# Routed experts behind a thresholded attention: rows stored unnormalized with their factors, low parts moved to GpSimd, a search with fewer steps per level, and a later turning of rows

## The chip, the cores and the metric

One Trainium2 chip, one of its cores. The metric is the device time of one execution in microseconds (us). Engines are named as the profile names them: PE is TensorE (PEld its weight loads), DVE is VectorE, ACT is ScalarE, POOL is GpSimd, SP is SyncE, which here only issues DMAs. Each engine runs its own instruction stream in order.

## The reference

```python
scores = scale * q @ k.T                                  # 8 batches, 8 heads, 576 rows, head size 64
scores = where(scores >= max(scores) - tau, scores, -1e9)
attn   = softmax(scores);  x = (attn @ v) as rows         # 4608 rows of 512
logits = x @ w_gate                                       # 8 experts
for idx in argsort(-logits.flatten()):                    # greedy, each expert takes at most 576 rows
    if row not assigned and expert not full: assign
out[mask_e] = relu(x[mask_e] @ w1[e]) @ w2[e]             # w1[e]: 512x1024, w2[e]: 1024x512
```

With 4608 rows and eight experts of 576 every expert ends full. The kernel finds, round by round, the expert that fills at the highest threshold, its 576 rows, and closes it.

## The kernel before

**Attention** (L23 to L328) goes through 32 pairs of heads of a batch: scores, maximum, exponential, mask with row sums, transposes, product with v. The result of a batch stays as XT (features by rows), not yet divided by the row sums; `rd_calc` and `rd_unit` form the reciprocals (RD). `xt_unit` (L202) turns one tile of 128 rows (64 for c=4) with four transposes on PE into a PSUM bank of `bank_v` (two banks), and `ev` (L209) multiplies each row's eight heads by their reciprocals and stores the tile in `xrows` in DRAM by SP. For batches 0 and 1 DVE multiplies from PSUM (L213). For the other six the ACT copies and POOL multiplies (L219), or, for the tile c=4, ACT does eight small scalings (L217). These 30 units run after the attention (L323 to L327): a loop that keeps a clock of its own puts one unit every XTY=1.05 into the streams, and between them the steps of the first expert's search.

**Router** (L370 to L576). A search level compares the best logit of each row with 32 (or 16) levels (`step_cmp`, L415; DVE), counts per expert on PE (`step_cnt`), flags the levels at which some expert is full (`step_flag`), and sums the flags on PE into the next lower bound (`step_n`, L437). There are seven levels, lv from -1 to 5. From lv 1 on a level adds a multiple of a step to the bound: tile E2, made by DVE from `st`, the bound and the sum in PSUM, is compared in the next level. `pick` and `pick2` find the expert: the one-hot matrix is masked, summed on DVE, summed over partitions on PE, and the first expert with a count of CAP or more is taken. `rank1`, `rank2`, `pack` give the list of rows (`idx`); `close` takes the expert and its rows out of the logits.

**Experts** (`moe`, L582). `run` holds jobs (generators) with due times; an expert's matmuls (`ffn`, L661) advance its clock, and whatever falls due is written into the streams between two matmuls. All numbers are split into a high part (fp32r) and the low rest, and three products are summed. Jobs of expert r are `w1_load` (L593: load, high part on ACT, low part w1l on DVE), `w2_load` (L617), `rows` (L634: gather of five tiles by POOL's indirect DMA after `idx`, then per tile four transposes on PE, high part xh on ACT, low part xl on DVE) and the search of the next expert (`place`, L704), which starts for r>2 once the second layer of expert r-3 is done. In `ffn` the first layer makes eight blocks of 128 features (PSUM, relu into `hf` on ACT, high part into H on ACT, low part in `low`, L678); the low part is on POOL for experts in LOWP=(0,1), else on DVE, and always on DVE for the last block. The second layer (L684) makes five row tiles, which POOL scatters to the output. For expert 0, `ffn` begins when half of the rows are turned ("half"), and its first block is made in two halves.

Constants of the schedule: GA (wait between gather and turning), RW (wait after each turned tile), LATS (allowance for a DVE result in a search step), each by expert.

Of the kernel before, what the change touches and what calls it, by code (L numbers as in the profile page):

```python
# [19 lines left out]
PPB=8; LTB=1; VTB=5; HOLD=1; CAPV=3.3; RATE=(2.4,2.4); NBO=2; XAC=(4,); NDEF=4; XTB=4; XTY=1.05; XT0=2.0; XRB=2  # L20


def attention(ctx, tc, qk, vl, tau, wgd, xrows, xts, Lg, nb_batches, ident, swap, R, after_first):  # L23
# [134 lines left out]
    RD={}  # L158
# [43 lines left out]
    def xt_unit(b,c):  # L202
        ps=bank_v([128,4,128])
        n=128 if c<4 else 64
        for j in range(4):
            T.transpose(ps[:n,j],XT[b][:,j,c*128:c*128+n],ident)
        if b<nb_batches-NDEF-NBO: xr=wk.tile([128,512],F32,name="xr",bufs=XRB)
        else: xr=wk.tile([128,2,S],F32,name="pp",bufs=PPB)[:,0,:512]
        def ev():  # L209
            src=RD[b][:,:,2*c:2*c+2] if c<4 else RD["m",b][0:64]  # L210
            src=src.unsqueeze(3).to_broadcast([n,4,2,64])
            xv=xr[:n].rearrange("p (j h d) -> p j h d",j=4,h=2); pv=ps[:n].rearrange("p j (h d) -> p j h d",h=2)
            if b<nb_batches-NDEF-NBO: V.tensor_tensor(xv,pv,src,op=ALU.mult)  # L213
            elif c in XAC:
                for j in range(4):
                    for h in range(2):
                        A.activation(xv[:,j,h],pv[:,j,h],AF.Copy,scale=RD[b][:n,j,2*c+h:2*c+h+1] if c<4 else RD["m",b][0:64,j,h:h+1])  # L217
            else:
                A.activation(xv,pv,AF.Copy); G.tensor_tensor(xv,xv,src,op=ALU.mult)  # L219
            nc.sync.dma_start(xrows[b*S+c*128:b*S+c*128+n,:],xr[:n])  # L220
        return ev
# [111 lines left out]
def const_arrays():  # L333
# [10 lines left out]
    put("lev",2.0**(1-5.0*np.arange(1,6)))  # L344
    put("io",np.arange(J+2)); put("io4",np.arange(J+2)/16)
# [24 lines left out]
class Router:  # L370
# [8 lines left out]
    def consts(s):  # L379
# [14 lines left out]
        s.cmp=t("cmp",[128,NC_*J],BF16); s.fl=t("fla",[128,1],BF16); V.memset(s.fl,0.0)  # L394
# [35 lines left out]
    def step_flag(s,lv):  # L430
# [4 lines left out]
        jk=s.wk.tile([32,8],F32,name="jka")  # L435
        V.tensor_scalar(jk,ps[0:32,0:8],CAP-0.5,None,op0=ALU.is_ge,op1=ALU.max,accum_out=s.fl[0:32])
    def step_n(s,B):  # L437
# [3 lines left out]
        E2=s.wk.tile([128,J+2],F32,name="E",bufs=3)  # L441
        ps=s.ps()
        if lv>0:
            s.T.matmul(ps[:,0:1],s.hb[:,lv-1:lv].to_broadcast([128,128]),s.fl,start=True,stop=True)
            if lv<5: V.scalar_tensor_tensor(E2,s.st[:,lv-1],B["lo"],ps[:,0:1].to_broadcast([128,J+2]),op0=ALU.add,op1=ALU.add)
            else: V.tensor_tensor(E2[:,:1],B["lo"],ps[:,0:1],op=ALU.add)
            return {"E":E2,"lo":E2[:,0:1],"lv":lv+1}
        n=ps[:,0:1]
        s.T.matmul(n,s.ones,s.fl,start=True,stop=True)
# [12 lines left out]
    def pick(s,E):  # L462

        V=s.V; wk=s.wk; lo=E["lo"]
        ge=wk.tile([128,NC_],BF16,name="ge"); s.ge=ge; V.tensor_scalar(ge,s.b,lo,None,op0=ALU.is_ge)
        V.tensor_tensor(s.oh,s.oh,ge.unsqueeze(2).to_broadcast([128,NC_,8]),op=ALU.mult)
        c8=wk.tile([128,8],BF16,name="c8"); s.c8=c8
        with s.nc.allow_low_precision(reason="counts up to 36 are exact"): V.tensor_reduce(c8,s.oh.rearrange("p c e -> p e c"),axis=AX.X,op=ALU.add)
    def pick2(s):
        V=s.V; wk=s.wk; ps=s.ps()  # L470
        s.T.matmul(ps[:,0:8],s.ones,s.c8,start=True,stop=True)
        f=wk.tile([128,8],F32,name="f8"); s.m=wk.tile([128,1],F32,name="m8")
        V.scalar_tensor_tensor(f,ps[:,0:8],CAP-0.5,s.w8,op0=ALU.is_ge,op1=ALU.mult)
# [63 lines left out]
    def phase(s,last=False):  # L537
# [21 lines left out]
        yield V.wait()  # L559
        held(0.13); s.pick2(); s.stage="pick"; s.rank1(E)  # L560
        yield V.wait()
        held(0.2); s.rank2()
    def pack(s,first):
# [4 lines left out]
        if first: s.warm(WARM[0])  # L568
        yield V.wait()
        held(0.7); s.compact(cps,poh,R)  # L570
        if first: s.warm(WARM[1])
        yield V.wait()
        held(0.5); s.gather4(cps)
        if first: s.warm(WARM[2])
        yield V.wait() if first else 0.35
        s.idx=s.compact2(cps)  # L576

LATS=[0.15,0.05,0.4]+[0.6]*5; FIX=(0.125,0.2)
GA=[7.0,5.5,7.5,9.0]; HALF=1; WARM=[20,4,50]
W1Y=5.0; L2O=(0,4,1,2,3); L2Z=1; HFB=3; RW=[0.2,0.6,1.0,2.0]; LOWP=(0,1); LPF=7; LOWT=1.4; PREPW=1; WLY=(1.0,1.0)  # L580

def moe(ctx,tc,R,start,xrows,w1,w2,out,ident):  # L582
# [10 lines left out]
    def w1_load(r,s):  # L593
        while r>0 and ("w1",r-1) not in done: yield 0.5
# [7 lines left out]
        s["w1h"]=w1p.tile([128,4,F],F32R,name="w1h"); s["w1l"]=w1p.tile([128,4,F],F32R,name="w1l")  # L602
        for k in range(4):
            t=s["w1s",k]
            if r==0:
                A.activation(s["w1h"][:,k],t,AF.Copy)
                while "idx" not in s: yield 0.25
                V.tensor_tensor(s["w1l"][:,k],t,s["w1h"][:,k].bitcast(F32),op=ALU.subtract)
                yield 1.1; continue
# [6 lines left out]
        done.add(("w1",r))  # L616
# [17 lines left out]
    def rows(r,s):  # L634
# [11 lines left out]
        for t in order:  # L646
# [10 lines left out]
            if t==1: done.add(("half",r))  # L657
# [165 lines left out]
```

## Time and profile before

| what | value |
| --- | --- |
| device time, three runs | 1034.92, 1032.56, 1034.87 us (median 1034.87) |
| the profiled execution | 1034.18 us, of it span 1032.4 us |
| busy PE / DVE / ACT / POOL | 980.9 / 776.4 / 640.7 / 323.7 us |
| mean granted PE clock | 0.976 |
| first matmuls of experts 0, 1, 2, 3 | 545.95, 618.10, 679.93, 739.28 us |
| last matmul | 1022.68 us |
| data moved by DMA | 113.03 MB, mean 109 GB/s |

The page gives busy time per engine and cuts the span into 40 slices. A window row says, for a stretch from a to b: its length, busy time of each engine with the number of instructions, the granted clock of PE, the share of the DMA engines and GB/s. A timeline row says: start, duration, engine, line, operation, written tile, read tiles, shapes, number of instructions merged; in brackets the idle time before it and what ended it. A group row says: line, engine, operation, tiles, shapes, count | busy time, mean duration in ns | idle time before them. Operations of DVE in the router and the experts all carry L366, the line of the helper that records them; they are told apart by their tiles.

### The profile page before, as it was taken

Reading aid. Unit: us, or ns where it says so; the run is one execution under the profiler, and the core shown is the slowest. Engines: PE = TensorE matmul, PEld = TensorE weight load, DVE = VectorE, ACT = ScalarE, POOL = GpSimd, SP = SyncE. Lnnn points to the kernel's source line nnn. Section 1 sums busy time; section 2 is a strip of 40 time slices with the busy share of each in tenths; the row PEclk is TensorE's granted clock in tenths of the full one; section 3 lists DMA queues with packets and bytes.
Section 4 is the critical chain, followed back from the end, with each engine's and each line's share of the span. In section 5 each row is a group of like instructions: output and inputs, shape, how many; then the busy total and the mean of one; then the engine's idle time right before and its main releaser. Section 6 shows DMA issues by size and latency. Waiting matters only on the chain. (4 is left out here: it accounts for less than half of the span.)

```text
span 1032.4 us, 24067 instructions
## 1 busy us (share of the span) xinstructions
PE 980.9 (95%) x9122; PEld 716.1 (69%) x9122; DVE 776.4 (75%) x2086; ACT 640.7 (62%) x1221; POOL 323.7 (31%) x485
## 2 busy tenths in 40 slices
PE   7999999999999999999768899999999999999996
PEld 4555555555555555555557779798897978889895
DVE  7999999999999999997677677767585676844230
ACT  6889888888888888886544235444352534445340
POOL 3333433333333333332653445312204021232201
PEclk9999999999999999999588999999999999999998
DMA  6321134232433222302563251504325051364101
GB/s 224 108 90 72 65 138 149 85 136 103 153 107 107 108 80 81 108 2 93 181 204 102 89 162 52 191 30 134 127 82 169 16 196 62 125 219 137 41 11 41
DMA packets 36003, 113.03 MB, mean 109 GB/s; under 512 B 4400, under 2 KB 5296, under 8 KB 35376
## 3 DMA queue, kind: packets, MB, share of 16 engines
q1 hardware_dynamic: 28496, 89.03, 24.3%
q0 software_dynamic: 5888, 18.88, 5.9%
q10 hardware_dynamic: 1504, 3.59, 1.1%
q8 instruction: 72, 1.18, 0.5%
q14 instruction: 43, 0.35, 0.1%
HBM read 89.19 MB, written 21.23 MB: 107 GB/s over the span
## 5 line engine op out<-in xcount | busy, mean ns | idle before, releaser
L76 POOL TENSOR_SCALAR nb<-nb,taub 128x1 f32<-128x1 f32 x288 | 147.4, 512 | 294.5 <-DVE z L75 223.4
L75 DVE TENSOR_SCALAR_CACHE_REDUCE z<-sc 128x576 f32<-128x576 f32 x288 | 205.9, 751 | 32.4 <-PE sc L70 31.0
L86 ACT ACTIVATE pp<-z,nb 128x576 f32<-128x576 f32 x256 | 187.3, 773 | 31.7 <-DVE z L75 30.3
L90 DVE SCALAR_TENSOR_TENSOR pp<-z,nb,pp 128x576 f32<-128x576 f32 x256 | 199.9, 813 | 0.3
L690 PE MATMUL pf<-w2h,H 128*128 128x512 f32 x576 | 196.1, 402 | 1.1 <-DVE H L366 1.1
L70 PE MATMUL sc<-qk 64*128 64x288 f32 (+1 forms) x1280 | 179.9, 426 | 2.1 <-DMA qk<-qk_dram 1.7
L145 PE MATMUL xo<-pt,vt 128*64 128x288 f32 x1024 | 151.9, 418 | 0.7 <-ACT xt L152 0.7
L114 ACT ACTIVATE pt<-tb 128x512 f32<-128x512 f32 x256 | 140.1, 594 | 13.9 <-PE tb L99 11.4
L99 PEld LDWEIGHTS tb<-ident,pp 64*128 64x128 f32 x2304 | 86.0, 139 | 71.6 <-ACT pt L114 16.7
L690 PE MATMUL pf<-w2l,H 128*128 128x512 f32 x320 | 128.2, 401 | 0.0
L697 POOL DMA_INDIRECT out_dram<-y,idx x40 | 41.9, 1048 | 265.9 <-ACT y L693 161.4
L690 PEld LDWEIGHTS pf<-w2h,H 128*128 128x128 f32 x576 | 106.3, 188 | 20.0 <-DVE H L366 1.5
L99 PE MATMUL tb<-ident,pp 64*128 64x64 f32 x2304 | 109.0, 230 | 10.1 <-ACT pt L114 6.0
L70 PEld LDWEIGHTS sc<-qk 64*128 64x128 f32 (+1 forms) x1280 | 94.4, 179 | 30.6 <-DVE pp L90 9.2
L670 PE MATMUL pf<-xh,w1h 128*128 128x288 f32 x512 | 113.5, 300 | 1.2 <-ACT xh L653 1.2
L670 PE MATMUL pf<-xh,w1l 128*128 128x288 f32 x512 | 113.9, 301 | 0.0
L670 PE MATMUL pf<-xl,w1h 128*128 128x288 f32 x512 | 113.3, 300 | 0.0
L676 ACT ACTIVATE hf<-pf 128x576 f32<-128x576 f32 x64 | 41.8, 652 | 105.7 <-PE pf L670 94.7
L145 PEld LDWEIGHTS xo<-pt,vt 128*64 128x64 f32 x1024 | 62.5, 136 | 63.5 <-issue 26.2
L693 ACT ACTIVATE y<-pf 128x512 f32<-128x512 f32 x40 | 23.9, 598 | 115.9 <-PE pf L690 99.3
L670 PEld LDWEIGHTS pf<-xh,w1h 128*128 128x128 f32 x512 | 83.1, 190 | 3.7 <-ACT xh L653 1.7
L670 PEld LDWEIGHTS pf<-xl,w1h 128*128 128x128 f32 x512 | 82.8, 189 | 0.2 <-DVE xl L366 0.2
(185 smaller groups left out, 1366.8 us busy)
## 6 DMA issues: line engine op xcount, KB each, us to landing
qk<-qk_dram SPq DMA_DIRECT2D x31, 1008.0 KB, 4.8
w2s<-w_dram SPq DMA_DIRECT2D x32, 512.0 KB, 5.6
w1s<-w_dram SPq DMA_DIRECT2D x28, 512.0 KB, 5.6
vt<-vl_dram SPq DMA_DIRECT2D x32, 320.0 KB, 5.5
xrows<-pp SPq DMA_DIRECT2D x24, 256.0 KB, 2.0
xts<-xt SPq DMA_DIRECT2D x2, 1152.0 KB, 5.2
pt<-xts SPq DMA_DIRECT2D x2, 1152.0 KB
xrows<-xr SPq DMA_DIRECT2D x8, 256.0 KB, 2.1
```

What stands on the lines that cost most here:

```text
L70: T.matmul(sc[o,f,:HS], kd["q",h][r,c], kd[k,h][r,:],start=True,stop=True)
L75: V.tensor_scalar(z,SC.pop(t)[:,:,:HS],-0.125,None,op0=ALU.mult,op1=ALU.min,accum_out=nb[:,0:1])
L76: G.tensor_scalar(nb[:,1:2],nb[:,0:1],taub[:,0:1],None,op0=ALU.add)
L86: A.activation(pview(t),ZB[t].rearrange("p a b -> p (a b)"),AF.Exp,bias=NBI[t][:,0:1],scale=-1.0)
L90: V.scalar_tensor_tensor(pv,ZB.pop(t).rearrange("p a b -> p (a b)"),NBI[t][:,1:2],pv,op0=ALU.is_le,op1=ALU.mult,accum_out=den_of(p)[:,p%4, ...
L99: g=slice(64*r,64*r+64); T.transpose(o[:,r],x[g],ident[g,g])
L114: A.activation(PT[p][:,i%2,:,(i//2)*128:(i//2+1)*128].rearrange("p k (r q) -> p r k q",r=2),tb,AF.Copy)
L145: T.matmul(xo[64*h:64*h+64,:HS],v[:,u,64*h:64*h+64],PT[p][:,h,u,q],start=(u==0),stop=False,skip_group_check=True)
L670: T.matmul(ps[:,h,:HS],s[w][:,k,f*128:(f+1)*128],s[x][:,k,h*HS:(h+1)*HS], start=(k==0 and j==0),stop=(k==3 and j==2))
L676: A.activation(hf,ps[:,:,:HS],AF.Relu)
L690: T.matmul(ps[:,0,:],H[:,f,c:c+128],s[w][:,f],start=(f==0 and j==0),stop=e)
L697: G.indirect_dma_start(out=out,out_offset=IOA(ap=s["idx"][:n,t:t+1],axis=0),in_=y[:n],in_offset=None)
```

## The change

- `xt_unit`: rows are stored as they are, 520 columns wide: 512 values and the row's eight reciprocals. Early batches: DVE copies from PSUM, POOL copies the factors. Others: two copies on ACT. POOL's multiplies and the small scalings are gone.
- `rows`: a gathered tile is multiplied by its factors, on DVE in place (for expert 0's tile of 64 rows by eight scalings on ACT), before it is turned. The scaling of tile i+1 is issued right after the turning of tile i.
- Search: from lv 2 on one `scalar_tensor_tensor` compares `st` plus the sum in PSUM with the logits, so E2 isn't formed; in its place the sum in PSUM is made of the flags of all levels so far (1 to 5 small matmuls). The bound is added to `st` once. After lv 5 the counts come with the flags, so that `pick` needs neither the masked one-hot matrix nor its sums (except for the last expert).
- Expert 0 and 1: expert 1's search starts while expert 0's rows are gathered and goes through two levels between the turnings; `close` is cut in two and stands within `pack` for experts 0 and 1; w1l of expert 0 is made after its rows, in four column pieces; the order of expert 0's products is by kind (w1h·xh, w1h·xl, w1l·xh).
- Constants: LOWP is (0,1,2,3,4,5); GA, RW and LATS as below.

```diff
+        early=b<nb_batches-NDEF-NBO
+        if early: xr=wk.tile([128,XW],F32,name="xr",bufs=XRB)
...
             src=RD[b][:,:,2*c:2*c+2] if c<4 else RD["m",b][0:64]
...
-            if b<nb_batches-NDEF-NBO: V.tensor_tensor(xv,pv,src,op=ALU.mult)
-            elif c in XAC:
...
+            if early:
+                V.tensor_copy(xv,ps[:n]); G.tensor_scalar(fv,src,1.0,0.0,op0=ALU.mult,op1=ALU.add)
             else:
-                A.activation(xv,pv,AF.Copy); G.tensor_tensor(xv,xv,src,op=ALU.mult)
+                A.activation(xv,ps[:n],AF.Copy); A.activation(fv,src,AF.Copy)
...
     def step_cmp(s,E):
+        if lv>1:
+            o=1 if lv<5 else 0
+            V.scalar_tensor_tensor(s.cmp...,s.st[:,lv-2,o:o+J]...,E["add"],s.b...,op0=ALU.add,op1=ALU.is_le)
+            return
...
     def step_flag(s,lv):
+        if lv==1: V.tensor_scalar(s.st,s.st,s.lo,None,op0=ALU.add)
...
     def step_n(s,B):
-            s.T.matmul(ps[:,0:1],s.hb[:,lv-1:lv].to_broadcast([128,128]),s.fl,start=True,stop=True)
-            if lv<5: V.scalar_tensor_tensor(E2,s.st[:,lv-1],B["lo"],ps[:,0:1].to_broadcast([128,J+2]),...)
+            for l in range(lv,0,-1):
+                k=32 if l==5 else 128
+                s.T.matmul(d,s.hb[0:k,l-1:l].to_broadcast([k,128]),s.jk[:,8:9] if l==5 else s.fl[:,l:l+1],start=(l==lv),stop=(l==1))
+            if lv<5: return {"add":d,"lv":lv+1}
+            s.T.matmul(ps[:,1:10],s.ones[0:32],s.jk,start=True,stop=True)
...
     def pick(s,E):
+        if "full" in E: return s.which(E["full"][:,1:9],E["full"][:,9:10])
...
-LATS=[0.15,0.05,0.4]+[0.6]*5; FIX=(0.125,0.2)
-GA=[7.0,5.5,7.5,9.0]; HALF=1; WARM=[20,4,50]
-...RW=[0.2,0.6,1.0,2.0]; LOWP=(0,1)...
+LATS=[0.15,0.12,0.25]+[0.35]*5; FIX=(0.125,0.2)
+GA=[5.0,6.5,11.0,12.0]; HALF=1; WARM=[20,4,50]
+...RW=[0.2,0.5,0.8,1.0]; LOWP=(0,1,2,3,4,5)...
...
     def w1_load(r,s):
+        if r==0:
+            for k in range(4):
+                A.activation(s["w1h"][:,k],s["w1s",k],AF.Copy); yield 1.1
+            done.add(("w1",0))
+            for a,b in ((0,1),(1,2),(2,4),(4,8)):
+                while ("row",0,1 if a==0 else 3) not in done: yield 0.1
+                o=slice(128*a,128*b)
+                for k in range(4):
+                    V.tensor_tensor(s["w1l"][:,k,o],s["w1s",k][:,o],s["w1h"][:,k,o].bitcast(F32),op=ALU.subtract)
+                    if a>1: yield 0.9 if a<4 else 2.0
+                for f in range(a,b): done.add(("w1l",f))
...
     def rows(r,s):
+        def scale(t):
+            if (r,t)==(0,4):
+                x=s["xg",t][:n]
+                for h in range(8): A.activation(x[:,64*h:64*h+64],x[:,64*h:64*h+64],AF.Copy,scale=x[:,D+h:D+h+1])
+                return
+            V.tensor_tensor(v,v,s["xg",t][:n,D:XW].unsqueeze(2).to_broadcast([n,8,64]),op=ALU.mult)
+        if r==0:
+            step0=R.phase(); R.ahead=step0
+            for _ in range(3): next(step0)
         yield GA[min(r,3)]
...
+            step(); scale(4); step(); scale(0); turn(4); step(); turn(0); step(); scale(1); low(4); step()
+            turn(1); low(0); step(2); scale(2); yield V.ease()
+            low(1); done.add("ahead"); yield 1.5
+            turn(2); yield 0.8
+            scale(3); low(2); yield 0.7
+            turn(3); low(3)
+            done.add(("x",0)); return
+        scale(order[0])
+        for i,t in enumerate(order):
+            turn(t)
+            if i<4: scale(order[i+1])
+            yield 0.8
+            low(t)
             yield RW[min(r,3)]
```

More of the change, by code (lines that the diff above doesn't have):

```diff
@@ L344, in const_arrays @@
     put("lev",2.0**(1-5.0*np.arange(1,6)))
+    lw=np.tile(2.0**(1-5.0*np.arange(1,6)),(128,1)); lw[0,4]=0; put("lew",lw)
     put("io",np.arange(J+2)); put("io4",np.arange(J+2)/16)
@@ L558, in phase, with pack @@
         s.pick(E)
-        yield V.wait()
-        held(0.13); s.pick2(); s.stage="pick"; s.rank1(E)
+        if last:
+            yield V.wait()
+            held(0.13); s.pick2()
+        s.stage="pick"; s.rank1(E)
         yield V.wait()
         held(0.2); s.rank2()
-    def pack(s,first):
+    def pack(s,first,alone):
         V=s.V; hib,prb=s.hib,s.prb; cps=s.cp()
@@ L568, in pack @@
         if first: s.warm(WARM[0])
+        if alone: s.close1()
         yield V.wait()
@@ L571, in pack @@
         if first: s.warm(WARM[1])
+        if alone: s.close2()
         yield V.wait()
@@ L593, in w1_load @@
     def w1_load(r,s):
-        while r>0 and ("w1",r-1) not in done: yield 0.5
+        while r>0 and ("w1a",r-1) not in done: yield 0.5
         q=nc.scalar if r==0 else nc.sync
@@ L602, in w1_load @@
         s["w1h"]=w1p.tile([128,4,F],F32R,name="w1h"); s["w1l"]=w1p.tile([128,4,F],F32R,name="w1l")
+        if r==0:
[9 more added lines that the diff above has]
+                for f in range(a,b): done.add(("w1l",f))
+            done.add(("w1a",0))
+            return
         for k in range(4):
             t=s["w1s",k]
[L605 to L609, printed above, removed]
             for c in range(2):
@@ L623, in w2_load @@
         yield 5.0
-        while ("w1",r) not in done or (r==0 and ("x",0) not in done) or (r>0 and ("l2",r-1) not in done): yield 0.5
+        while ("w1a",r) not in done or (r==0 and ("x",0) not in done) or (r>0 and ("l2",r-1) not in done): yield 0.5
         s["w2h"]=wk.tile([128,8,D],F32R,name="w2h"); s["w2l"]=wk.tile([128,8,D],F32R,name="w2l")
@@ L657, in rows, with step @@
             if t==1: done.add(("half",r))
+        if r==0:
+            def step(n=1):
+                for _ in range(n): next(R.ahead)
+            step(); scale(4); step(); scale(0); turn(4); step(); turn(0); step(); scale(1); low(4); step()
[11 more added lines that the diff above has]
+            low(t)
             yield RW[min(r,3)]
@@ L665, in ffn @@
             for hs in (((0,),(1,)) if r<=HALF and f==0 else ((0,1),)):
-                if hs==(1,): yield None
-                for k in range(4):
-                    for j,(w,x) in enumerate((("w1h","xh"),("w1h","xl"),("w1l","xh"))):
-                        for h in hs:
-                            T.matmul(ps[:,h,:HS],s[w][:,k,f*128:(f+1)*128],s[x][:,k,h*HS:(h+1)*HS],
-                                     start=(k==0 and j==0),stop=(k==3 and j==2))
-                        if not (k==3 and j==2): yield 0.125*len(hs)
+                if hs==(1,): yield ("x",r)
+                ops=[(k,j) for j in range(3) for k in range(4)] if r==0 else [(k,j) for k in range(4) for j in range(3)]
+                for i,(k,j) in enumerate(ops):
+                    w,x=(("w1h","xh"),("w1h","xl"),("w1l","xh"))[j]
+                    if r==0 and (k,j)==(0,2): yield ("w1l",f)
+                    for h in hs:
+                        T.matmul(ps[:,h,:HS],s[w][:,k,f*128:(f+1)*128],s[x][:,k,h*HS:(h+1)*HS],start=(i==0),stop=(i==11))
+                    if i<11: yield (0.25 if (r,f)==(0,0) else 0.125)*len(hs)
             two=lambda a: a.rearrange("p (a b) -> p a b",a=2)
@@ L721, in steps @@
                     jobs.append([clk[0],w1_load(r,s)]); jobs.append([clk[0]+0.1,w2_load(r,s)])
-            yield from steps(start[0] if r==0 else R.phase(r==7))
-            if r==0:
+            yield from steps(start[0] if r==0 else R.ahead if r==1 else R.phase(r==7))
+            if r<2:
                 yield from packing(r,s)
-                yield 2.3; R.close(); yield 1.4
+                while "ahead" not in done: yield 0.1
             else:
@@ L750, in moe @@
         for d in ffn(r,st[r]):
-            while d is None and ("x",r) not in done:
-                now+=0.25; run(now)
-            if d is None: continue
+            if type(d) is tuple:
+                while d not in done:
+                    now+=0.25; run(now)
+                continue
             held[0]=0.0; now+=d; run(now); now+=held[0]; clk[0]=now
@@ L792, in build @@
         dr=ctx.enter_context(tc.tile_pool(name="dr",bufs=1,space=bass.MemoryType.DRAM))
-        xrows=dr.tile([8*S,512],F32,name="xrows")
+        xrows=dr.tile([8*S,XW],F32,name="xrows")
         xts=dr.tile([8,128,4,S],F32,name="xts")
```

79 lines of the change are left out of this document (44 added, 35 removed).

## The prediction

> **What bounds the kernel now.** I read the page's slices first, then windows cut at the stage borders, then the waits and the order of time between the stages.
>
> ```profile
> span 1032.4 us, 24067 instructions
> PE   7999999999999999999768899999999999999996
> PEclk9999999999999999999588999999999999999998
> 487.35:526.95 39.60, 27.32 (x220) 21.86 (x220) 26.67 (x60) 24.03 (x72) 27.78 (x24) 0.70 0.48 170
> 526.95:534.00 7.05, 5.44 (x57) 4.92 (x57) 4.40 (x16) 0.27 (x1) 0.00 (x0) 0.59 0.61 191
> 534.00:553.40 19.40, 12.77 (x105) 11.59 (x103) 13.92 (x27) 7.26 (x10) 6.32 (x6) 0.71 0.69 230
> 553.40:618.10 64.70, 59.87 (x456) 49.70 (x456) 45.98 (x114) 24.37 (x48) 28.53 (x25) 1.00 0.30 99
> 618.10:1023.07 404.97, 402.99 (x2865) 353.50 (x2863) 239.95 (x601) 171.97 (x337) 93.97 (x92) 1.00 0.31 104
> ```
>
> A window row gives its length, then busy time of PE, PEld, DVE, ACT and POOL, then granted clock, DMA share and GB/s. TensorE fills the attention stage and the experts from 618 on (402.99 of 404.97 us). Work there is worth time only if it is TensorE's. The hole is the middle, 66 us from the first late row unit (487.35) to the first finished feature block of expert 0 (553.40), where the clock too is at 0.59 to 0.71. The middle is a serial chain: seven search levels, pick, rank, gather, turning. The change works mostly there.
>
> **Late rows and the first search.**
>
> ```profile
> 493.08 0.21 PE L428 MATMUL sc<-oh,cmp 128*128 128x32 bf16 x2 [1.78 <-DVE cmp L366]
> 498.76 1.09 PE L206 MATMUL xo<-ident,xt 128*128 128x128 f32 x4
> L219 POOL TENSOR_TENSOR pp<-pp,rd 128x512 f32<-128x512 f32 x24 | 27.8, 1175 | 11.4 <-ACT pp L219 10.9 <-DVE cn L366 0.3
> 495.67 0.95 DVE L366 TENSOR_SCALAR E<-cst,sm 128x34 f32<-128x34 f32 x1
> 553.37 0.24 DVE L366 TENSOR_SCALAR E<-cst,sm 128x34 f32<-128x34 f32 x1
> L366 DVE TENSOR_TENSOR cmp<-b,E 128x1152 bf16<-128x1152 f32 x4 | 7.3, 1813 | 0.1
> 622.60 1.36 DVE L366 TENSOR_TENSOR cmp<-b,E 128x1152 bf16<-128x1152 f32 x1
> 519.84 2.25 DVE L366 TENSOR_TENSOR cmp<-b,E 128x1152 bf16<-128x1152 f32 x1
> 523.70 0.15 DVE L366 TENSOR_TENSOR E<-E,sc 128x1 f32<-128x1 f32 x1 [0.38 <-PE sc L444]
> 524.17 1.19 DVE L366 TENSOR_TENSOR oh<-oh,ge 128x288 bf16<-128x288 bf16 x1
> 526.40 0.17 DVE L366 SCALAR_TENSOR_TENSOR f<-rps,w8b 128x8 f32<-128x8 f32 x1 [0.35 <-PE rps L471]
> 526.80 0.15 DVE L366 TENSOR_SCALAR e<-m 128x1 int32<-128x1 f32 x1
> L219 ACT ACTIVATE pp<-xo 128x512 f32<-128x512 f32 x24 | 14.1, 597 | 12.6 <-PE xo L206 8.7 <-issue 3.1 <-PE sc L444 0.5
> L217 ACT ACTIVATE pp<-xo,rm 64x64 f32<-64x64 f32 x48 | 10.3, 307 | 2.7 <-PE sc L444 1.5 <-PE xo L206 0.6 <-POOL pp L219 0.6
> ```
>
> The same search instruction costs 0.95 us while GpSimd multiplies rows and 0.24 us later; the wide compare 1.81 against 1.36. The change takes all 24 multiplies (27.8 us) off GpSimd, so the search runs at the later durations. ScalarE trades eight small scalings per last tile for one copy, and adds a factor copy of 32 bytes a row, which I put at 0.22 us by the 64x64 row (10.3 us for 48): 30 x (0.60 + 0.22) = 24.6 us, against 24.4 now. No gain, no loss there; 0.82 us per unit is the pace ScalarE allows.
>
> A level now: the one from 519.84 takes 4.05 us to the end of E (523.85). With a 1.41 us compare (1.36 and 0.05 for the extra operand) and E dropped, 3.1 remain; I take 3.55, because units stand in TensorE's order between count, flag and sum. Working it forward from 487.35: six units, then the first count at +3.9 (now 493.08, +5.7); the next level 3.95, as it still has its four small operations; five at 3.55; from the last count to the expert number 3.3 (count, cast, flag, sums, then five short DVE operations, without oh, the count after it and a sum on TensorE, which stand from 524.17 to 526.40 today); 1.2 for banks that wait for ScalarE. That is 30.1 against 39.6: **-9.5 us**. Bounds: -11 (no such waits) and -4, if TensorE stays at half clock. That condition needs the clock's windows:
>
> ```profile
> 490.62:494.03 3.41, 1.63 (x23) 1.00 0.73 275
> 514.50:517.92 3.42, 3.42 (x19) 0.50 0.47 152
> 518.00:521.33 3.33, 2.11 (x26) 1.00 0.49 182
> 524.75:528.17 3.42, 0.52 (x3) 1.00 0.72 255
> ```
>
> The clock switches on a grid of 3.41 us: after a window with 1.63 us busy it fell to half, after 2.11 of 3.33 it stayed, after a full one it rose. So the border lies between 48% and 63%. In my forward schedule TensorE is busy two thirds or more of each level at full clock, so it should not fall at 494 as it does now. At half clock 30 units of about 1.0 us (1.09 at 498.76) and seven levels of about 1.2 us of TensorE fill 38 us by themselves, and only the pick is saved, with some of the waits.
>
> The Trainium skill's page "TensorE: Matmul & The Clock Gate" (Part 1: The HAM clock gate) gives the same window, 3413 ns, but has the clock drop after an idle window; this trace drops it after one that was 48% busy, so the measurement decides. By the page's rule alone the late stage would keep its clock even more surely, and the sum would stand.
>
> **From expert number to the first feature block.**
>
> ```profile
> 533.83 0.17 DVE L366 SCALAR_TENSOR_TENSOR idx<-cps,ih 128x5 int32<-128x5 f32 x1
> 539.45 0.43 PE L650 MATMUL pt<-ident,xg 64*128 64x64 f32 x4 [2.33 <-ACT w1h L606]
> 540.81 0.65 PE L650 MATMUL pt<-ident,xg 128*128 128x128 f32 x4 [0.93 <-DMA xg<-xrows,idx]
> 540.36 1.22 DVE L366 TENSOR_TENSOR w1l<-w1s,w1h 128x1024 fp32r<-128x1024 f32 x1
> 545.95 0.61 PE L670 MATMUL pf<-xh,w1h 128*128 128x288 f32 x1 [0.69 <-ACT xh L653]
> 553.69 0.65 ACT L676 ACTIVATE hf<-pf 128x576 f32<-128x576 f32 x1 [3.33 <-PE pf L670]
> L366 DVE TENSOR_TENSOR xl<-pt,xh 128x512 fp32r<-128x512 f32 (+1 forms) x40 | 25.4, 635 | 26.3 <-ACT xh L653 24.3 <-issue 1.9
> ```
>
> Rank and index keep their 7.05 us; the closing of the logits moves in, and its second half (0.9 us) exceeds DVE's gap before idx: +0.2. Row tiles land at +5.4 and +6.8 after idx whatever is done. New on the path are the scalings: eight on ScalarE for the 64-row tile (1.7 us, so it is turned at +7.2, not +5.4), then one of 0.64 on DVE per tile, the price of the xl row, which has the same size. Between them DVE runs expert 1's first two levels, while the w1l subtractions (four of 1.22) move behind the turning. Placed in order, tile 1 is turned at +10.5, the first matmuls go at +12.5 (now +12.0), but their xl halves wait for DVE until +14.8, and the second half for tile 3 until +20: block 0 ends at +21.2 instead of +19.4 (its relu comes at 553.69). Together **+2.0** (from -1, if DVE fits better, to +4). The loads of w1 are issued at the same distance from the expert number, on ScalarE's queue; SP's row writes carry 2080 instead of 2048 bytes a row, and land well before the gather that needs them.
>
> **Rest of expert 0.** TensorE is idle 4.8 of the 64.7 us, mostly for expert 1's search, its gather, and a low part that DVE did late. Expert 1 is two levels ahead after the change and its gather falls earlier. I take **-3.0** (bounds -4.8 and +1, as w2's casts now begin behind w1l).
>
> **Experts 1 to 7.**
>
> ```profile
> 594.03 0.59 PE L518 MATMUL cps<-ob,zz 128*128 128x10 bf16 x16
> L680 POOL TENSOR_TENSOR H<-hf,H 128x512 fp32r<-128x512 f32 (+1 forms) x14 | 14.3, 1042 | 12.3 <-ACT H L677 12.3
> L366 DVE TENSOR_TENSOR H<-hf,H 128x512 fp32r<-128x512 f32 x100 | 41.0, 452 | 23.9 <-ACT H L677 23.4 <-issue 0.5
> 714.24 0.99 POOL L640 DMA_INDIRECT xg<-xrows,idx  x1 [31.37 <-PE pf L690]
> 719.66 0.92 POOL L640 DMA_INDIRECT xg<-xrows,idx  x1 [0.30 <-issue]
> ```
>
> *Matmuls:* a search issues 16 small sums in place of 5, and the pick's goes. At 0.037 each (16 with their own weights in 0.59) that is 0.4 less 0.18, for six searches +1.4. *Low parts:* DVE loses 4 experts x 7 blocks x 2 x 0.45 = 25 us and gains 35 scalings x 0.64 = 22. DVE's load is level, and TensorE sees neither directly. *The new wait:* each turning stands in TensorE's queue behind a scaling in DVE's, and behind it stand the second layer's matmuls. Nothing like it is in the trace; nearest is the xl row, with 0.64 for one. Fully hidden it costs 0, fully exposed 35 x 0.64 = 22. DVE is busy 240 of 405 us, and a scaling is issued right behind the turning before it, which leaves it about 1.5 us; but each expert's first is issued with no lead. I take 4 (0.4 on each first, 0.04 on the others). *Gaps:* TensorE's idle time there is 2.0 now; shorter levels may save 0.9. Sum **+4.5** (from -1 to +12, where nearly half of the scalings show).
>
> **Sum.** -9.5 + 2.0 - 3.0 + 4.5 = -6.0 against the profiled execution's own 1034.18 (span 1032.4 and 1.8 around it): 1028.2. The median of the runs shown is 1034.87, so I say **1028**.
>
> **Rivals.**
>
> 1. *The late stage stays at half clock*: -4 instead of -9.5, so 1033.5. For: the clock sits at 0.50 there today. Against: the waits for cmp that emptied the window before 494 come from DVE operations that GpSimd stretched. Chance 0.13.
> 2. *Turning waits for the scalings*: near the whole 22 us at the turnings instead of 4, so 1046, slower than before. It decides when DVE's work per turned tile (0.64 + 0.64 and what the search and w1l put there) exceeds the tile's spacing. For: spacing shrinks to 0.8 + 0.8 or 1.0 us in the order written; DVE then has only 0.4 spare. Against: DVE's 35% idle time, much of it in front of xl (24.3 us for xh). Chance 0.08.
> 3. *GpSimd's queue*: low parts take 14.3 us per seven blocks, a gather 6.3 more (714.24 to the end of its fifth, 720.58), beside some 27 us of layer one. If a gather falls into its last blocks, the low parts come about 2 us late in four experts: 1036. Chance 0.05.
> 4. *The fused compare runs at half rate*: four levels at +1.2, 1033.
>
> ```profile
> L90 DVE SCALAR_TENSOR_TENSOR pp<-z,nb,pp 128x576 f32<-128x576 f32 x256 | 199.9, 813 | 0.3
> ```
>
> That row is the same kind of instruction with two f32 operands in SBUF, at 0.81 us for 576 columns: for 1152 that gives 1.6 at most, not 2.6. Chance 0.04. The rule behind it is in the Trainium skill, "Vector Engine (DVE) Microarchitecture Reference", Points that are easy to get wrong: such an instruction with two non-bf16 SBUF sources halves its throughput; the row contradicts it.
>
> 5. *Everything fits*: no waits at the turning, expert 0 without gaps: 1017 to 1022. Chance 0.15.
>
> The forecast case, 1022 to 1033, holds 0.55.
>
> **How the numbers follow.** About 0.3% (3.1 us) is what a measurement of this kernel can tell from no change. Faster than 1031.8: 0.50 of the forecast's 0.55, all of case 5, and 0.07 of the rivals near the border: 0.72. Within: the rest of the forecast, most of cases 1, 3 and 4: 0.19. Slower: case 2 and the tail of 3: 0.09. The range 1017 to 1036 leaves out case 2 and tails.
>
> **What would show it.** Right: L219 no longer on POOL, E at 0.25 and cmp near 1.4 before 520, clock 1.00 there, expert number at about 517.5 and idx at 524.7; block 0 done 21 us later. Wrong: clock 0.50 from 494; waits of PE pt on DVE in the tens of microseconds; waits of PE on POOL's H; a fused compare of 2.5 us.

## The result: 1046.0 us, and the profile after

The changed kernel takes 1046.01 us (median of 4 runs, 1042.01 to 1048.01) against 1034.8 for the kernel before: a ratio of 1.0109, 95% interval 1.0092 to 1.0125. It is slower, by 1.1%. The forecast was 1028, and the range ended at 1036. The profiled execution has a span of 1046.2 us against 1032.4; it is the slowest of the four, 2.0 us above their median, so sums read from its trace come out somewhat larger than the difference of the medians.

From the page of the kernel after: the span, and the two rows of the slices that were shown of before.

```profile
span 1046.2 us, 24220 instructions
PE   7999999999999999998789999989989899899996
PEclk9999999999999999999889999999999999999998
```

The hole in the middle is narrower than before, but the experts behind it now have eights where they had nines. The windows at the stage borders (length, busy time of PE, PEld, DVE, ACT and POOL, granted clock, DMA share, GB/s) give the sizes. The borders are the first late row unit, the expert number, `idx`, the first relu, the first matmul of expert 1, and that of expert 6; behind the last the matmuls end.

```profile
486.75:511.79 25.04, 20.43 (x230) 16.12 (x229) 15.64 (x55) 19.25 (x59) 0.00 (x0) 1.00 0.74 267
511.79:519.31 7.52, 4.75 (x58) 4.25 (x59) 5.66 (x22) 1.04 (x3) 0.00 (x0) 0.69 0.65 220
519.31:539.85 20.54, 15.86 (x129) 13.81 (x128) 15.03 (x45) 8.33 (x18) 6.82 (x6) 0.70 0.65 209
539.85:601.88 62.03, 58.62 (x427) 50.40 (x426) 45.63 (x102) 25.05 (x49) 26.14 (x25) 0.97 0.31 104
601.88:931.72 329.84, 311.70 (x2302) 268.02 (x2301) 216.33 (x488) 127.85 (x250) 134.45 (x136) 0.98 0.34 113
931.72:1036.57 104.85, 104.85 (x629) 94.73 (x627) 33.87 (x66) 43.89 (x87) 12.57 (x13) 1.00 0.14 47
```

The same two last stretches of the kernel before:

```profile
618.10:918.79 300.69, 298.71 (x2237) 259.08 (x2236) 208.90 (x540) 128.03 (x250) 74.35 (x73) 1.00 0.36 119
918.79:1023.07 104.28, 104.28 (x629) 94.42 (x627) 31.05 (x61) 43.94 (x87) 19.63 (x19) 1.00 0.18 59
```

Expert 1 starts at 601.88 instead of 618.10, 16.2 us earlier. Experts 1 to 5, those during which another expert is still searched, then take 329.84 us instead of 300.69: 29.2 us more. Experts 6 and 7 together differ by 0.6. TensorE idles 329.84 - 311.70 = 18.1 us in the five experts, where it idled 2.0; the other 13 us are busy time, in part at a lower clock (0.98 against 1.00). The POOL column is the one that changed most: 134.5 us busy against 74.4.

What TensorE waited for from 601.88 on (total, times, longest):

```profile
PE rps L438 <- DVE cn L364: 6.2, 5, 2.1
PE pt L698 <- DVE xg L364: 5.9, 4, 2.2
PE cps L528 <- DVE R L364: 2.1, 3, 1.0
PE cps L534 <- DVE ob L364: 1.2, 2, 1.0
```

None of the waits is for POOL. Nearly all are for DVE, and they are spread over the search (cn), the turning (xg) and the list of rows (R, ob), so no single step explains them. The stretches of DVE's and POOL's own rows do. Around 747 us, in layer one of expert 3, DVE makes the list of rows and POOL makes a low part:

```profile
747.67 1.62 DVE L364 TENSOR_TENSOR th<-pih,hib 128x720 bf16<-128x720 bf16 x1
749.33 0.98 DVE L364 TENSOR_TENSOR R<-th,ihl 128x720 bf16<-128x720 bf16 x2
```
```profile
747.56 1.92 POOL L746 TENSOR_TENSOR H<-hf,H 128x512 fp32r<-128x512 f32 x2 [1.81 <-ACT H L743]
```

`th` is as large as one of the two `R` behind it, which take 0.98 together, yet it takes 1.62: it ends when POOL's pair has nearly ended. `R` comes late, and TensorE waits 0.78 us for it.

### The profile page after: what moved, and what is told of

It reads as the page before. It is cut to its first block, busy times and chain, and to the rows that moved or that the text cites. A ratio compares the mean times of both kernels' runs of the same rounds, so it can differ in the third digit from the quotient of the medians.

```text
span 1046.2 us, 24220 instructions
## 1 busy us (share of the span) xinstructions
PE 987.9 (94%) x9192; PEld 720.4 (69%) x9192; DVE 777.6 (74%) x2046; ACT 637.9 (61%) x1217; POOL 351.0 (34%) x527
## 4 chain that ended last, share of the span: by engine, by line
PE 67%; DVE 16%; ACT 8%; issue 5%; DMA 2%; another core or an unknown queue 1%; DVEq 0%; POOLq 0%; POOL 0%; SPq 0%; ACTq 0%
PE pf L756 19%; PE pf L737 13%; PE xo L145 10%; PE sc L70 8%; PE tb L99 8%; ACT pp L86 3%; PE xo L150 2%; DVE z L75 2%; ACT pt L114 2%; PE pt L698 2%; DVE pp L90 2%; DVE cmp L364 2%; ACT pt L116 2%; DVE w2l L364 1%; PE xo L206 1%
## 5 line engine op out<-in xcount | busy, mean ns | idle before, releaser
L756 PE MATMUL pf<-w2h,H 128*128 128x512 f32 x576 | 198.2, 408 | 0.0
L114 ACT ACTIVATE pt<-tb 128x512 f32<-128x512 f32 x256 | 140.1, 594 | 13.8 <-PE tb L99 11.2
L756 PE MATMUL pf<-w2l,H 128*128 128x512 f32 x320 | 130.4, 408 | 0.0
L763 POOL DMA_INDIRECT out_dram<-y,idx x40 | 45.3, 1134 | 242.5 <-ACT y L759 205.0
L756 PEld LDWEIGHTS pf<-w2h,H 128*128 128x128 f32 x576 | 109.1, 193 | 19.6
L737 PE MATMUL pf<-xh,w1h 128*128 128x288 f32 x512 | 111.4, 304 | 0.1
L737 PE MATMUL pf<-xh,w1l 128*128 128x288 f32 x512 | 111.0, 303 | 0.0
L737 PE MATMUL pf<-xl,w1h 128*128 128x288 f32 x512 | 109.7, 301 | 0.7 <-DVE xl L364 0.7
L746 POOL TENSOR_TENSOR H<-hf,H 128x512 fp32r<-128x512 f32 x84 | 82.4, 1002 | 69.2 <-ACT H L743 69.2
```

The lines of the kernel that those rows point to most:

```text
L114: A.activation(PT[p][:,i%2,:,(i//2)*128:(i//2+1)*128].rearrange("p k (r q) -> p r k q",r=2),tb,AF.Copy)
L737: T.matmul(ps[:,h,:HS],s[w][:,k,f*128:(f+1)*128],s[x][:,k,h*HS:(h+1)*HS],start=(i==0),stop=(i==11))
L746: for l,h,c0,c1 in a: (G if r in LOWP and f<LPF else V).tensor_tensor(l,hf[:,:,c0:c1],h.bitcast(F32),op=ALU.subtract)
L756: T.matmul(ps[:,0,:],H[:,f,c:c+128],s[w][:,f],start=(f==0 and j==0),stop=e)
L763: G.indirect_dma_start(out=out,out_offset=IOA(ap=s["idx"][:n,t:t+1],axis=0),in_=y[:n],in_offset=None)
```

## Experiments

Three theories were put against each other. **G**: GpSimd's low parts of experts 2 to 5, by its queue or by holding VectorE back. **S**: the scalings ahead of the turnings. **L**: the shorter pauses in the search.

**Each part undone alone.** The first run:

```diff
-LOWP=(0,1,2,3,4,5)
+LOWP=(0,1)
```

> The changed kernel with one thing undone: low parts on GpSimd for experts 0 and 1 only, as before. Experts 1 to 5 lost 29.7 us against before (3.8, 8.0, 6.9, 7.5, 3.0 and 0.5), experts 6 and 7 nothing. Theory G (GpSimd's low parts hold VectorE back and stand around its gather): experts 2 to 5 give back most of their 25.4 us, the time falls from 1046 to about 1025, the waits of TensorE for the cast cn behind a gather (2.04, 2.11 and 1.57 us) go, and the half-clock windows behind them too. Theory S (the scalings ahead of the turnings): nothing of that, or worse, since VectorE takes 28 low parts (25 us) more: 1046 to 1052. Theory L (levels placed closer together): little, 1040 to 1046.

Measured: 1028.84 us (ratio 0.9947, 0.993 to 0.9963), 17.2 us less than the changed kernel. The waits for cn all but vanish and no half-clock window is left in experts 1 to 5, although DVE has 28 low parts more to make. What TensorE still waits for:

```profile
PE pt L698 <- DVE xg L364: 7.7, 5, 1.8
PE cps L528 <- DVE R L364: 0.3, 1, 0.3
PE rps L438 <- DVE cn L364: 0.2, 1, 0.2
```

Theory G holds for most of the loss. Experts 2 to 5 (from first matmul to first matmul) took 238.9 us before and 264.2 after; with the low parts undone they take 247.5, so 16.7 of 25.3 us come back. After, and with the low parts undone:

```profile
667.52:931.72 264.20, 248.56 (x1804) 214.51 (x1803) 169.17 (x381) 102.21 (x200) 107.84 (x110) 0.97 0.35 115
```
```profile
663.92:911.43 247.51, 240.90 (x1804) 208.48 (x1802) 168.59 (x437) 102.63 (x200) 58.48 (x53) 1.00 0.36 123
```

These windows start 3.6 us apart, although up to there the two kernels issue the same instructions in the same order on every engine. That difference is no work of the low parts; the last section shows where it arises.

The groups of DVE in both kernels, between 602 and 930 us (busy time, mean ns of one, idle time before), show where the low parts act. First after, then with the low parts undone:

```profile
L364 DVE TENSOR_TENSOR w2l<-w2s,w2h 128x512 fp32r<-128x512 f32 x40 | 36.1, 925 | 2.3 <-ACT w2h L660 2.3
L364 DVE TENSOR_TENSOR xl<-pt,xh 128x512 fp32r<-128x512 f32 x20 | 13.7, 685 | 4.9 <-ACT xh L699 4.8
L364 DVE TENSOR_TENSOR R<-th,ihl 128x720 bf16<-128x720 bf16 x12 | 9.2, 803 | 0.2
```
```profile
L364 DVE TENSOR_TENSOR w2l<-w2s,w2h 128x512 fp32r<-128x512 f32 x47 | 34.6, 738 | 20.3 <-ACT w2h L660 20.3
L364 DVE TENSOR_TENSOR H<-hf,H 128x512 fp32r<-128x512 f32 x38 | 26.1, 687 | 10.9 <-ACT H L743 10.6
L364 DVE TENSOR_TENSOR xl<-pt,xh 128x512 fp32r<-128x512 f32 x20 | 13.8, 688 | 6.0 <-ACT xh L699 6.0
L364 DVE TENSOR_TENSOR R<-th,ihl 128x720 bf16<-128x720 bf16 x12 | 7.0, 620 | 0.2
```

The same subtraction w2l takes 925 ns in the mean instead of 738, `R` 803 instead of 620. `xl`, of the same size but with one operand in PSUM, is unchanged (685 and 688). If the lower quartile of each form in the second kernel is taken as its normal time, and all that is over it by more than 60 ns is added up over 600 to 930 us, DVE's instructions are stretched by 27.0 us after, 5.6 with the low parts undone, and 5.8 in the kernel before. The Trainium skill states this in "SBUF — State Buffer", section "Who interferes with whom": a VectorE instruction with two inputs in SBUF and a GpSimd instruction that reads SBUF exclude each other, and the one that comes second waits until the other has ended. The rows agree, `xl` included.

**The pauses.**

```diff
-LATS=[0.15,0.12,0.25]+[0.35]*5
+LATS=[0.15,0.12,0.4]+[0.6]*5
```

> The changed kernel with the planned pause after each search step put back to 0.4 us for expert 2 and 0.6 us from expert 3 on (now 0.25 and 0.35). Theory L (levels closer together make TensorE wait for VectorE's steps, and put the gather into layer one): the waits for cn and R shrink and the time falls to 1030 to 1038. Theory G: at most 3 us, 1043 to 1046. Theory S: no change.

Measured: 1033.0 us (ratio 0.9984, 0.9972 to 0.9996), 13.0 less. Theory L's number; but the stretch of DVE's instructions is still 27.8 us. So stretching alone does not set the price: what meets it does.

**The turning's pauses.**

```diff
-GA=[5.0,6.5,11.0,12.0]; RW=[0.2,0.5,0.8,1.0]
+GA=[5.0,5.5,7.5,9.0]; RW=[0.2,0.6,1.0,2.0]
```

> The changed kernel with the turning's pauses put back: 5.5, 7.5 and 9.0 us after the gather in place of 6.5, 11 and 12, and 0.6, 1.0 and 2.0 us between tiles in place of 0.5, 0.8 and 1.0. Theory S: wider spacing hides the scalings, but they start earlier and so nearer to the gather's landing; the waits of the turning for xg (6.9 us in experts 1 to 5) change by some 3 us, time 1042 to 1048. Theories G and L: no change beyond 3 us.

Measured: 1045.39 us. The time stays and the waits change kind: those for xg rise from 5.9 to 13.6 us, more than theory S put down, and those for cn fall from 6.2 to 0.2. The later turning is neither cause nor cure.

**No scalings.** `scale` returns at once for experts 1 to 7; the run leaves their normalization out.

> The changed kernel without the scalings for experts 1 to 7: their rows stay unnormalized, 35 VectorE operations less. Theory S (the turnings wait for the scalings): the 6.9 us of waits for xg go, with the half-clock window at 904 behind one of them, and the time falls by 9 us or more, to 1037 or below; at its most, near the whole loss of 29.7 us. Theories G and L: the time falls by the 6.9 us of visible waits at most, and the waits for cn behind the gather stay at about 2 us each.

Measured: 1041.27 us, 4.7 less than after: within what theories G and L allowed, and half of what theory S asked for. The waits for xg are gone, and against theories G and L those for cn too, but others of 12.7 us, for cmp, stand in their place. This run has the clearest picture of the cause; one of the two longest instructions of DVE and what POOL did then:

```profile
688.91 5.22 DVE L364 SCALAR_TENSOR_TENSOR jk<-cst,rps,E 128x34 f32<-128x34 f32 x1 [1.04 <-PE rps L461]
```
```profile
688.14 0.20 POOL L673 COPY ei<-e 128x1 int32<-128x1 int32 x1
688.28 6.07 POOL L747 TENSOR_TENSOR H<-hf,H 128x512 fp32r<-128x512 f32 x8
```

`jk` works on 34 elements a row and elsewhere takes 0.26 us. Here it starts 0.6 us into a run of eight subtractions on GpSimd and ends 0.2 us before that run does. The eight stand back to back because they had piled up behind the gather, which ends with the copy at 688.14. So `jk` was held for nearly the whole run of eight, not for one subtraction. (At 748.36 another `jk` took 7.01 us, within ten subtractions.) One such row holds up a level of the search, and TensorE's next matmul in its queue with it: the count behind this one waited 3.93 us for cmp.

**GpSimd's operations without their results.** DVE makes the low parts as in the first run; in experts 2 to 5 GpSimd makes the same number of subtractions at the same places, into a tile that nobody reads:

```diff
+ if 2<=r<=5 and f<LPF:
+   for h,n in ((hT,512),(hL,64)): G.tensor_tensor(two(dum[:,:n]),h.bitcast(F32),h.bitcast(F32),op=ALU.subtract)
```

> Low parts on GpSimd for experts 0 and 1 only; in experts 2 to 5 VectorE makes them, and GpSimd makes subtractions of the same sizes at the same places into a tile that nobody reads (its inputs are the high parts). Nothing waits for GpSimd's results here. Theory C (GpSimd's operations themselves hold VectorE's instructions back): VectorE's stretched instructions return to 20 us or more and the time rises from 1028.8 to 1040 or above. Theory Q (the harm is in its queue: low parts behind the gather, buffers that come free late): 1028 to 1031, with VectorE's instructions unstretched.

Measured: 1044.55 us (ratio 1.0093, 1.0075 to 1.0111), 15.7 more than the run without them. Nothing waits for the tile, so the stretch is the operations' own: 28.6 us, with DVE's low parts at 869 ns instead of 687:

```profile
L364 DVE TENSOR_TENSOR H<-hf,H 128x512 fp32r<-128x512 f32 x33 | 28.7, 869 | 0.9 <-ACT H L744 0.8
```
```profile
L749 POOL TENSOR_TENSOR dum<-H 128x512 f32<-128x512 f32 x28 | 35.2, 1258 | 43.4 <-ACT H L744 43.4
```
```profile
669.72:926.06 256.34, 243.69 (x1803) 210.01 (x1802) 190.15 (x437) 102.56 (x200) 108.45 (x109) 0.99 0.35 119
```

Not all of the 15.7 us is theirs, though. Up to the first subtraction into the tile, at 675.0, this kernel too issues what the first run issues, but for one clearing of the tile, and yet expert 2 starts 5.8 us later (669.72 against 663.92). The last row is its experts 2 to 5: 256.3 us against 247.5. So in the traces the operations alone make 8.8 us, about half of the 16.7 that the low parts make there; what makes the other half was not shown apart. The waits for cn belong to it (6.2 us after, 0.5 here) and the half-clock windows of experts 2 to 5 (four after, one here).

**Low parts alone, in the kernel before** (`LOWP=(0,1)` to `(0,1,2,3,4,5)` there):

> The kernel before with one thing added: low parts on GpSimd for experts 0 to 5. Theory I (hidden by the longer pauses of the kernel before): VectorE's instructions stretch by 20 us or more in experts 2 to 5, the time stays within 5 us of before, 1032 to 1040. Theory P (costs by itself): 1047 to 1052.

Measured: 1041.83 us (ratio 1.0062, 1.004 to 1.0084): slower by 6.6, between the two forecasts, with theory I's stretch (28.8 us by the same sum). The same move costs less than half of the 17.2 us that it costs in the changed kernel. That the longer pauses are the reason is not shown: in the changed kernel with long pauses the move even saves 4.0 us (the table below).

**Both undone**, low parts and pauses:

> The changed kernel with both undone: low parts on GpSimd for experts 0 and 1 only, and pauses of 0.4 and 0.6 us in the search. Either alone brought 1028.8 and 1033.0. Theory I (the two hurt together: GpSimd's low parts make single VectorE instructions 1.1 to 1.3 us longer, 27 us in experts 1 to 5 in either placing, and TensorE only sees it where the levels stand close): no further gain, 1027 to 1031. Theory P (each costs by itself, about 17 and 13 us): 1016 to 1020.

Measured: 1036.97 us. Neither theory: the two undone together are slower than either alone.

| low parts on GpSimd | short pauses | long pauses |
|---|---|---|
| experts 0 to 5 | 1046.0 | 1033.0 |
| experts 0 and 1 | 1028.8 | 1037.0 |

Each variant places every step anew, and as far as the trace tells single meetings decide. The profiled execution, the fastest of its ten, is 6.2 us above that of the first run. Of these, 3.9 stand in expert 4 (66.2 us against 62.3 from first relu to first relu), with one wait of 3.13 us for xg and the half-clock window behind it, and 2.1 in expert 0, where the instructions are still the same and a cast cn came 2.3 us late at 583.14. Neither the pauses nor the low parts have a fixed price that adds up.

**The gather out of layer one**, all low parts still on GpSimd:

```diff
 def rows(r,s):
+    while r>1 and ("l1",r-1) not in done: yield 0.5
```

> The changed kernel, all low parts of experts 0 to 5 on GpSimd, with each gather from expert 2 on held back until layer one of the expert before has been issued, so that no low part stands behind it on GpSimd and no count of a search falls beside it in layer one. Theory C (the operations themselves stretch VectorE's instructions): the stretched time stays at 20 us or more and the time at 1042 or above. Theory Q (the gather in layer one does the harm: waits for cn behind it of 2.04, 2.11 and 1.57 us, the half-clock windows that follow, low parts one after the other): 1033 to 1038.

Measured: 1036.53 us, 9.5 less than after, with a stretch of 25.9 us still there (the profiled execution took 1032.8). Both theories have half of it: the stretched instructions remain, but where no gather stands in layer one no low parts pile up behind it, the waits for cn fall to 0.2 us, and no half-clock window is left there.

**Towards a better kernel.** The first scaling of each expert had no lead over its turning; with the low parts undone it got one:

```diff
-        scale(order[0])
+        scale(order[0]); yield 1.5
```

> Low parts on GpSimd for experts 0 and 1 only, and the first scaling of each expert planned 1.5 us ahead of its turning. In the run with those low parts undone TensorE waited 1.13, 1.80, 1.81, 1.64 and 1.34 us for xg in experts 2 to 6, each at the expert's first turning, 7.7 us in all. Theory S (what is left of the loss is the first scaling): these waits go, 1021 to 1024. Rival: the scaling is late because VectorE is busy or the gather lands late, and the waits stay or come back elsewhere: 1027 to 1030.

Measured: 1026.91 us (0.9921, 0.9904 to 0.9937). The 7.7 us of waits fall to three of 0.2 to 0.3, and experts 2 to 5 take 1.1 to 2.1 us less each (from first relu to first relu), but expert 0 takes 3.0 more, with a cast cn that came 2.4 us late at 584.15, and expert 1 1.2 more. Then, with that lead, fewer low parts on GpSimd:

```diff
-LOWP=(0,1)
+LOWP=(0,)
```

> Low parts on GpSimd for expert 0 alone, with the same lead. Theory C: expert 1 falls from 65.8 to about 61 us, 1021 to 1024, and the kernel without any on GpSimd is faster still. Rival (expert 0 needs GpSimd's help): this one is the fastest of all, 1020 to 1024, and the one without is slower than it.

Measured: 1025.33 us (1025.15 to 1026.07; ratio 0.9917, 0.99 to 0.9933), the lowest time: 9 us below before and 20.7 below the change. By its ratio it cannot be told from the run with experts 0 and 1 there; expert 1 fell to 63.1 us, not to 61. And with none:

> No low parts on GpSimd at all, and the first scaling of each expert 1.5 us ahead of its turning. With experts 0 and 1 on GpSimd and this lead the time was 1026.9, and experts 0 and 1 took 65.9 and 65.8 us against 60.3 to 61.2 for experts 2 to 4. Theory C (GpSimd's operations hold VectorE back wherever they stand): expert 1 falls to about 61 and expert 0 by up to 3 us, 1018 to 1023. Rival: in expert 0 VectorE is full (w1's and w2's low parts, expert 1's search) and 14 low parts more make TensorE wait there: 1026 to 1032.

Measured: 1039.35 us, 14 us more than with expert 0's seven low parts on GpSimd. The rival had the direction, but not the size, and its reason does not show: expert 0 takes 66.3 us against 65.9, and DVE is busy for 46.6 us of it. The loss comes later. Expert 1's rows are turned from 593.6 on instead of 586.1, and expert 1 takes 71.7 us against 63.1: expert 2's rows, turned during it, come when layer two has run out of matmuls. Why the steps fall so late was not tested.

**A pause beside the gather.** From the best kernel, the search stands still for 7 us from each gather on:

```diff
+        if r>0: V.after(clk[0]+7.0)
```

> Low parts on GpSimd for expert 0 alone, the first scaling 1.5 us ahead, and the search planned to stand still for 7 us from each gather of experts 1 to 7. In the run without the pause (1025.3) TensorE waited for cn beside a gather 1.08, 0.34, 0.61 and 1.00 us in experts 1 to 4. Theory H (a count that ends beside the gather reaches VectorE late, whatever else goes on): these waits go and the time falls by 2 to 4 us, 1021 to 1024. Rival (the waits come from VectorE's own work, or the pause only moves the search onto the turnings): no gain or a loss, 1025 to 1030, with waits of other kinds in their place.

Measured: 1058.77 us. The waits for cn beside the gather went, as theory H has it, but the search moved onto the turnings, which then came behind the end of layer two: at least 14.7 us of waits at `pt`, and clock lost. The rival's price, far above its estimate; what the waits for cn cost by themselves this run cannot tell.

## Why the prediction was wrong, step by step

The terms as forecast, and as the two traces have them (in us of the profiled executions):

| term | forecast | measured | from |
|---|---|---|---|
| before the late rows | 0 | -0.6 | 486.75 against 487.35 |
| late rows and first search | -9.5 | -14.6 | expert number 511.79 against 526.95 |
| expert number to first relu | +2.0 | +1.3 | 28.06 against 26.74 |
| rest of expert 0 | -3.0 | -2.4 | 62.03 against 64.41 |
| experts 1 to 7 | +4.5 | +30.0 | 444.3 against 414.3 to the end of the span |

They add up to +13.8, the difference of the spans. **The first search** was right in mechanism and too small in size. Two levels after the change, their compares 3.06 us apart; then a window with the granted clock of the stage:

```profile
501.40 1.42 DVE L364 SCALAR_TENSOR_TENSOR cmp<-st,sc,b 128x1152 bf16<-128x1152 f32 x1 [0.39 <-PE sc L454]
504.46 1.42 DVE L364 SCALAR_TENSOR_TENSOR cmp<-st,sc,b 128x1152 bf16<-128x1152 f32 x1 [0.41 <-PE sc L454]
```
```profile
494.03:514.66 20.63, 15.27 (x188) 12.28 (x185) 12.75 (x44) 13.15 (x41) 0.00 (x0) 1.00 0.75 266
```

The prediction worked out 3.1 and then took 3.55, for row units between the steps, and added 1.2 for banks. At full clock the units cost nothing there. The compare took 1.42, as forecast (1.41, of which no row had shown the 0.05 for the extra operand), so rival 4 fell; the clock stood at 1.00 in the late stage, so rival 1 fell. The gain even passed the bound of -11. Two readings of the prediction are off and move little: the level from 519.84 to 523.85 is 4.01 us long, not 4.05, and DVE's idle share behind 618, by the row 239.95 of 404.97, is 41%, not 35%.

**Expert number to first block** and **the rest of expert 0** came within 0.7 us of their terms, the second by chance: with the low parts of later experts undone, where expert 0's instructions are the same, it is -5.6 (58.79 us against 64.41). A cast at 582.97 that came late and a half-clock window behind it make the difference (the last section).

**Experts 1 to 7** is the step that failed, and in it the sentence "DVE's load is level, and TensorE sees neither directly". It counted the 25 us that DVE no longer spends and priced 28 pairs of subtractions on GpSimd at nothing, as if the two engines were independent. The prediction held the evidence: its first term rests on a search instruction that took 0.95 us beside GpSimd's multiplies and 0.24 without. It booked the gain where GpSimd's work leaves DVE, and not the loss where the same kind of work joins it. GpSimd's pairs of experts 1 to 5 take 68 us:

```profile
L746 POOL TENSOR_TENSOR H<-hf,H 128x512 fp32r<-128x512 f32 x35 | 48.9, 1396 | 46.7 <-ACT H L743 46.7
L746 POOL TENSOR_TENSOR H<-hf,H 128x64 fp32r<-128x64 f32 x35 | 19.0, 543 | 0.0
```

DVE's instructions lost 21 us to the 28 pairs that were added (27.0 less 5.6), and without these pairs the kernel is 17.2 us faster. The operations alone, with nobody reading their results, make about half of the loss in experts 2 to 5; for the rest the step from them to TensorE's waits stays open.

The 29.2 us in experts 1 to 5 are made up so: TensorE idles 16.2 us more. Behind four windows with such idle time the clock stands at half for 3.41 us, as here (a window, and the one behind it):

```profile
763.84:767.25 3.41, 1.48 (x18) 1.17 (x16) 0.08 (x1) 0.58 (x2) 3.10 (x5) 1.00 0.73 214
767.25:770.66 3.41, 3.24 (x15) 3.00 (x16) 1.32 (x8) 0.41 (x1) 1.80 (x4) 0.50 0.61 221
```

At 3.1 to 3.4 us busy and half speed each costs some 1.6 us, 6.5 together, by this estimate. Sums and turnings take some 3 us more of busy time (forecast: +1.4 for the sums). About 3.5 us stay unassigned. Not all of the 29.2 is the low parts': without them the five experts take 312.4 us, 11.7 more than before, of which 7.7 are waits for xg.

**The rivals.** The second named 1046, which is the time, but not the cause: it put 22 us on the scalings, and without them the kernel still takes 1041.3. The third had the place right, the gather in layer one's last blocks, and its 8 us are near the 9.5 that moving the gather gives back; but no low part came late to TensorE. It is DVE that stood behind the low parts piled up. The case that won, GpSimd holding VectorE back, was not among the rivals at all.

Without the added low parts the kernel takes 1028.8, the forecast, but by luck. In its trace the expert number comes 15.1 us earlier than before, where 9.5 was forecast, and the rest of expert 0 gives 5.6, where 3.0 was; experts 1 to 7 cost 13.7, where 4.5 was (428.0 us against 414.3), and 7.7 of that are waits for xg, where 4 were put down.

## What to carry to other kernels

Before moving work to another engine, look in the same trace for what that engine's work does to its neighbour: price the stretched instructions, not only the time that moves. In an order written out by hand, idle gaps of TensorE come from single meetings of two streams, and one of some 2 us within a clock window was followed by half speed here in most cases; so judge a change with each part undone alone, and do not add the parts' gains. Compare two traces first where both kernels issue the same instructions: what differs there (2.9 to 5.8 us here) is not the change. The same move can help in one stage (14 us by expert 0's low parts) and harm in the next.

## What the runs showed of the hardware

A cast of 32 elements a row was held back beside a gather, and the cause stays open. In the kernel after, the count for `cn` ended at 764.42 by its rows, and DVE, idle since 763.63, read it 2.75 us later:

```profile
764.03 0.39 PE L432 MATMUL rps<-oh,cmp 128*128 128x32 bf16 x9
765.86 0.20 POOL L673 COPY ei<-e 128x1 int32<-128x1 int32 x1
767.17 0.19 DVE L364 CAST cn<-rps 128x32 fp32r<-128x32 f32 x1 [3.54 <-remote]
```

This happened four times in the kernel after (at 582.97, 702.44, 767.17 and 831.83), each time 1.1 to 1.25 us after the copy that follows a gather. GpSimd's subtractions are no condition of it: it stands in the kernel with none of them, too (count, copy, cast there):

```profile
587.47 0.39 PE L432 MATMUL rps<-oh,cmp 128*128 128x32 bf16 x9
588.32 0.19 POOL L673 COPY ei<-e 128x1 int32<-128x1 int32 x1
590.89 0.19 DVE L364 CAST cn<-rps 128x32 fp32r<-128x32 f32 x1 [4.05 <-remote]
```

Other counts beside gathers were read at once: in the kernel after one of 643.06 was read at 643.49, with its gather's copy at 645.14. And the same instruction does both. Up to 669 us the kernel after and the first run, with low parts undone, issue the same; here are the count and the cast in expert 0, first after, then in the first run:

```profile
580.23 0.39 PE L432 MATMUL rps<-oh,cmp 128*128 128x32 bf16 x9
582.97 0.19 DVE L364 CAST cn<-rps 128x32 fp32r<-128x32 f32 x1 [2.70 <-remote]
```
```profile
580.58 0.39 PE L432 MATMUL rps<-oh,cmp 128*128 128x32 bf16 x9
581.01 0.19 DVE L364 CAST cn<-rps 128x32 fp32r<-128x32 f32 x1 [0.40 <-PE rps L432]
```

With the half-clock window behind it the late cast makes most of the 2.9 us by which expert 1 starts later after (601.88 against 599.00). The run with subtractions into an unread tile has two such casts before its first subtraction, at 527.04 and 584.93. How often it happens in executions that were not profiled is not known, so a difference of some 3 us between two runs need not come from their edits.

In experts 1 to 5 of the kernel after the clock fell behind windows with 1.66, 1.48, 1.43 and 1.38 us busy of 3.41; the other three are these:

```profile
698.98:702.39 3.41, 1.66 (x15) 0.90 (x13) 0.00 (x0) 2.85 (x6) 3.10 (x4) 1.00 0.78 223
835.52:838.93 3.41, 1.43 (x14) 0.69 (x13) 3.41 (x9) 1.02 (x3) 0.00 (x0) 1.00 0.95 323
900.37:903.78 3.41, 1.38 (x8) 1.25 (x9) 3.41 (x6) 1.86 (x5) 2.14 (x3) 1.00 0.99 362
```

In the first of them DVE is idle throughout, waiting for a count; in the last two it is busy throughout, and late. The border that the prediction worked out, between 48% and 63% busy, does not hold. In expert 0 of the kernel after the clock fell behind a window with 1.91 us busy (56%); in the first run it stayed behind one with 1.60 (47%). Each window with the one behind it, after and then the first run:

```profile
582.91:586.32 3.41, 1.91 (x16) 1.58 (x17) 2.85 (x8) 0.90 (x2) 0.00 (x0) 1.00 0.78 256
586.32:589.74 3.42, 3.42 (x12) 2.72 (x12) 2.72 (x8) 1.97 (x4) 0.75 (x1) 0.50 1.03 383
```
```profile
706.13:709.54 3.41, 1.60 (x10) 1.03 (x9) 3.30 (x10) 0.00 (x0) 0.00 (x0) 1.00 0.98 348
709.54:712.95 3.41, 3.41 (x27) 2.67 (x26) 2.63 (x6) 1.98 (x4) 0.00 (x0) 1.00 0.80 303
```

The busy share of a window alone does not tell whether the clock falls; what else decides stays open.
